# Weight-slice scales from sums of squares on ScalarE, and the last y tiles kept in PSUM, in an attention and two-MoE kernel

## The chip, the cores and the metric

The kernel runs on one core of one Trainium2 chip. The metric is the device time of one execution in microseconds; lower is better. Five engines work side by side, each through its own instructions in a fixed order: PE (matmuls), DVE (vector), ACT (scalar), POOL (general) and SP, which here only starts DMAs. An instruction that waits stops everything behind it on its engine.

## The reference

Attention over 4 batches of 8 heads (576 positions, width 64), then two feed-forward layers on 2304 tokens of width 512:

```python
def _moe_ref(x, w_in, w_out, s, b):            # w_in 512x2048
    r = np.maximum(x @ w_in, 0.0)
    return ((s * (r * r) + b) @ w_out).astype(np.float32)

def _moe2_ref(x, w_a, w_b, w_out):             # w_a, w_b 512x1536
    return (((x @ w_a) * (x @ w_b)) @ w_out).astype(np.float32)

def reference(...):                            # attention -> x [2304, 512]
    x = _moe_ref(x, **moe_kwargs)
    return _moe2_ref(x, **moe2_kwargs)
```

## The kernel before

**Order.** The kernel is not run through loops on the chip. At build time each step is declared with `op(engine, cost, prio, fn, r, w, ...)`: an engine, a planned duration, a due time (smaller is earlier), what it reads and writes. A list scheduler (`Plan`) then fixes the order of each engine from these costs, due times and the number of free buffers. A planned duration that differs from the real one makes no error, only an order that fits less well.

**Stages.** Tokens form 9 chunks of 256. Attention and the first MoE run chunk by chunk up to about 498 us of the span. `last_two` then runs the first MoE for the last two chunks together: 16 slices of hidden units (hh, L987) are folded into four output tiles `yy0` to `yy3` in PSUM (L999), each 128 x 512, where 256 columns belong to chunk 7 and 256 to chunk 8. In the kernel before, a tile is read by DVE for its largest absolute value (L1006), copied to SBUF (L1012, two on ACT and two on DVE), stored to DRAM (L1015) and loaded again where it is used (L1200, L1237).

**The first half of MoE 2** (L1246, from 586 us) computes x @ w_a and x @ w_b in six slices `i` of 256 hidden units. For each slice, each of the two weights `m` and each of two blocks `j` of four chunks, `group` runs seven products, as in Strassen's scheme: 11, d2, d1, 21, d3, d4, 22. A product is `mm6`, six matmuls of 128x512 in fp16. The products share three PSUM banks: b1 takes 11 and then 21 on top, b2 takes d2, d3, d4, and b3 takes d1, 22. Between two products on one bank, a partial result must have been read from it: ACT copies b1 to `su` (L1298), DVE adds b2 to it (L1284, `su`, `u3`, `at_all`), for m = 1 DVE also multiplies (L1291). The product that comes next on the bank waits for that read. The ninth chunk goes without Strassen: `conv` runs two halves of 12 smaller matmuls for each slice and weight (banks `bc`). Of x, the kernel keeps pieces `x011` to `x0d4` (block 0), `x111` to `x1d4` (block 1) and `xc` (ninth chunk), each an fp16 high part (ACT, L1179) and a low part (DVE, L1180) scaled by `xsc`; the differences for block 1 are made on POOL (L1209). `x_scale` gets `xsc` through one small matmul `xbank` (L1101) and five tiny DVE operations (L1105 to L1109).

**Weight slices.** `w2_slice` prepares 18 slices of 1 MB: 12 of w_a and w_b (names like `raw2_03`: weight 0, slice 3) and 6 of w_out (`raw2_o1`). Each is loaded (L459) and decoded in three passes over 128x1024: a Prelu on ACT (L463), a shift, on DVE (L472) for one half of the slices and on ACT (L468) for the other, and a combination on DVE (L474). Then come sums of blocks (L1137), and for the 12 slices the largest absolute value on DVE (L1143), a matmul `wbank` over the partitions in PE's own queue (L1147), two tiny DVE operations (L1151, L1152), and the splits into `wa` and `ws` (ACT L1160, DVE L1166).

**The second half** (`pb`, L1490, from 849 us) multiplies the products a*b, reloaded from DRAM, by w_out.

Of the kernel before, what the change touches and what calls it, by code (L numbers as in the profile page):

```python
# [238 lines left out]
def fused_kernel(  # L239
# [845 lines left out]
    def x_scale(z, t_bank, pos):  # L1085
        i, sc = 10 + z, xsc[:, z]
        both = [(ymax_b, c) for c in ((0, 1, 2, 3) if z == 2 else (4, 5, 6, 7))]

        def tail():
            c0 = 0 if z == 2 else 4  # L1090
            nc.vector.tensor_reduce(out=ymax[:, 9:10], in_=ymax[:, c0 : c0 + 4], axis=AX.X, op=ALU.max)
            if z == 2:
                nc.vector.tensor_tensor(out=ymax[:, i : i + 1], in0=ymax[:, 9:10], in1=ymax[:, 9:10], op=ALU.mult)
            else:
                nc.vector.tensor_tensor(out=ymax[:, 9:10], in0=ymax[:, 9:10], in1=ymax[:, 9:10], op=ALU.mult)
                nc.vector.tensor_tensor(out=ymax[:, i : i + 1], in0=ymax[:, 9:10], in1=ymax[:, 8:9], op=ALU.add)
# [603 lines left out]
```

## Time and profile before

| what | value |
|---|---|
| median of 3 runs | 989.39 us (985.68 to 991.02) |
| the profiled execution's own time | 988.24 us |
| its span | 986.3 us |
| TensorE clock granted over the span, share of full | 0.996 |
| attention and first MoE of chunks 0 to 6 | 0 to about 498.7 us |
| first MoE of the last two chunks | 498.7 to 586.5 us |
| MoE 2, first half (L1246) | 586.5 to 849.0 us |
| MoE 2, second half (L1490, L1550) | 849.0 to 986 us |

The profile is one execution. Times in its rows are microseconds from the start of the span; the device time has 1.9 us around the span. In a row of a timeline, what stands in square brackets is the idle time of the engine just before, and the instruction whose end released it.

### The profile page before, as it was taken

The page shows a single profiled execution, that of the slowest core. Times are in us where ns is not written, and L with a number is a line of the kernel's source. Part 1 is how long each engine was busy: PE and PEld are TensorE (multiplying, and loading weights), DVE is VectorE, ACT ScalarE, POOL GpSimd, SP SyncE. Part 2 cuts the span into 40 slices and gives each one's busy share as a digit, 9 for nine tenths or more (in the row PEclk, how much of TensorE's full clock was granted, in tenths as well). Part 3 has the DMA queues.
Part 4 walks back from the last instruction along what each step waited for, and adds up shares of the span by engine and source line. Part 5 has one row for each costly group of instructions (what it writes and reads, how often), then busy time and mean ns, then how long its engine had stood idle before and what let it go on. Part 6 is the DMA issues. An engine that isn't in the chain of part 4 may idle for free.

```text
span 986.3 us, 16813 instructions
## 1 busy us (share of the span) xinstructions
PE 945.5 (96%) x6361; PEld 765.0 (78%) x6361; DVE 743.6 (75%) x1221; ACT 548.0 (56%) x1009; POOL 159.4 (16%) x228
## 2 busy tenths in 40 slices
PE   5799999999999999999999998998999999999998
PEld 4698998999999999999978873554554544688888
DVE  6878665677978888888487548789687886878852
ACT  4788984567878787877464424343253431334431
POOL 4112003210201102003031004124132411000000
PEclk9999999999999999999999999999999999999999
DMA  8969555447788778776541113547256657976012
GB/s 251 225 162 242 178 205 126 92 133 157 159 175 153 172 150 187 139 166 137 137 160 59 43 49 106 175 156 261 98 197 210 244 203 282 395 291 236 22 67 104
DMA packets 161552, 165.34 MB, mean 168 GB/s; under 512 B 115264, under 2 KB 126272, under 8 KB 155584
## 3 DMA queue, kind: packets, MB, share of 16 engines
q1 hardware_dynamic: 161472, 164.28, 58.4%
q8 instruction: 50, 0.82, 0.3%
q14 instruction: 30, 0.25, 0.1%
HBM read 100.44 MB, written 37.52 MB: 140 GB/s over the span
## 4 chain that ended last, share of the span: by engine, by line
PE 73%; DVE 12%; DMA 8%; issue 3%; ACT 2%; POOL 1%; SPq 1%; DVEq 0%; POOLq 0%; ACTq 0%
PE h L931 14%; PE y L951 13%; PE b L1246 12%; PE pb L1490 11%; PE yy L999 4%; PE av L593 4%; PE hh L987 4%; PE s L643 2%; PE s L829 2%; PE bc L1246 2%; PE pbc L1550 2%; DMA tr<-hl 2%; DVE at_all L1291 1%; DMA raw<-in_w_dram 1%; DMA raw<-in_w2ab_dram 1%
## 5 line engine op out<-in xcount | busy, mean ns | idle before, releaser
L951 PE MATMUL y<-g,w 128*128 128x256 f32 x1344 | 181.3, 286 | 2.0 <-ACT p L659 2.0
L931 PE MATMUL h<-x_all,w 128*128 128x256 f32 x1344 | 179.1, 287 | 1.4 <-ACT x_all L604 0.6
L931 PEld LDWEIGHTS h<-x_all,w 128*128 128x128 f32 x1344 | 168.9, 194 | 2.7 <-ACT x_all L604 0.8
L951 PEld LDWEIGHTS y<-g,w 128*128 128x128 f32 x1344 | 167.7, 192 | 3.9 <-ACT p L659 2.2
L1246 PEld LDWEIGHTS <-wa 128*128 128x128 f16 x720 | 70.2, 99 | 64.1 <-issue 9.4
L1246 PEld LDWEIGHTS <-ws 128*128 128x128 f16 x576 | 56.3, 98 | 69.8 <-issue 4.3
L553 ACT ACTIVATE hl<-p,rc 128x256 f16<-128x256 f32 (+3 forms) x128 | 64.7, 557 | 20.2 <-DVE rc L570 9.7
L1246 PE MATMUL b<-x,wa 128*128 128x512 f16 x288 | 69.8, 379 | 1.2 <-ACT su L1298 0.7
L555 DVE SCALAR_TENSOR_TENSOR hl<-p,rc,hl 128x256 f16<-128x256 f32 (+3 forms) x128 | 66.4, 565 | 3.3 <-ACT hl L553 3.2
L881 ACT ACTIVATE r<-h 128x512 f32<-128x512 f32 x56 | 33.1, 591 | 52.6 <-PE h L931 52.5
L593 PE MATMUL av<-tr,vt 128*64 128x320 f16 (+4 forms) x800 | 48.1, 275 | 10.1 <-DMA tr<-hl 9.5
L593 PEld LDWEIGHTS <-vt 128*64 128x64 f16 (+1 forms) x800 | 40.8, 117 | 18.3 <-issue 7.2
L1246 PE MATMUL b<-x1d,ws 128*128 128x512 f16 x216 | 51.7, 379 | 2.1 <-DVE su L1284 1.5
L1490 PE MATMUL pb<-g,wo 128*128 128x512 f32 x216 | 50.8, 390 | 1.6 <-DVE g L1438 1.6
L643 PE MATMUL s<-kq 66*128 66x256 f32 (+1 forms) x128 | 42.4, 458 | 10.5 <-POOL vt L374 7.7
L1246 PE MATMUL b<-x0d,ws 128*128 128x512 f16 x216 | 51.3, 379 | 0.0
L892 DVE SCALAR_TENSOR_TENSOR r<-r,sb_s 128x512 f32<-128x512 f32 x40 | 30.1, 752 | 27.4 <-ACT r L881 27.0
L1298 ACT COPY su<-b 128x512 f32<-128x512 f32 x24 | 14.0, 583 | 64.7 <-PE b L1246 57.0
L1490 PEld LDWEIGHTS pb<-g,wo 128*128 128x128 f32 x216 | 40.4, 188 | 10.4 <-DVE g L1438 2.1
L987 PE MATMUL hh<-x_all,w 128*128 128x512 f32 x192 | 46.3, 391 | 1.1 <-DMA x_all<-xl_dr 1.1
L999 PE MATMUL yy<-gg,w 128*128 128x512 f32 x192 | 45.8, 389 | 0.0
L1284 DVE TENSOR_TENSOR su<-b,su 128x512 f32<-128x512 f32 x48 | 32.7, 685 | 15.8 <-PE b L1246 15.5
(408 smaller groups left out, 1853.5 us busy)
## 6 DMA issues: line engine op xcount, KB each, us to landing
raw<-in_w_dram SPq DMA_DIRECT2D x16, 1024.0 KB
raw<-in_w2ab_dram SPq DMA_DIRECT2D x12, 1024.0 KB
ab_dr<-at_all SPq DMA_DIRECT2D x24, 512.0 KB
R<-ab_dr SPq DMA_DIRECT2D x24, 512.0 KB
wo<-wo_dr SPq DMA_DIRECT2D x12, 1024.0 KB
rk<-in_k_dram SPq DMA_DIRECT2D x16, 576.0 KB
raw_o<-in_w2o_dram SPq DMA_DIRECT2D x6, 1024.0 KB
wo_dr<-wao SPq DMA_DIRECT2D x24, 256.0 KB
```

What stands on the lines that cost most here:

```text
L553: nc.scalar.activation(o, i_, AF.Copy, scale=r_)
L555: nc.vector.scalar_tensor_tensor(out=o, in0=i_, scalar=r_, in1=place()[:, k0:k1, 0, :cols], op0=ALU.mult, op1=ALU.subtract)
L593: nc.tensor.matmul(ap.t[64 * h : 64 * h + 64, :w], vap(j, h, vi), t[:, j, a, h, :w], start=j == 0 and m == 0, stop=j == nkt - 1 and m == l ...
L643: nc.tensor.matmul(o, qt[:66, x, h, ti * P : (ti + 1) * P], kt[:66, x, h, :w], start=True, stop=False)
L881: op(ACT, 0.49, e, lambda: nc.scalar.activation(r.t.rearrange("p a n -> p (a n)"), hp.t, AF.Relu), r=[hp], w=[r], late=0.1)
L931: nc.tensor.matmul(o, w[:, wi, c, :], x_t[ck, c].t[:, xi], start=m == 0, stop=m == 3 * KC - 1)
L951: nc.tensor.matmul(o, w1_t[2 * fp + j].t[:, 1, wi, e * P : (e + 1) * P], g.t[:, gi, j], start=fp == 0 and e % 2 == 0 and j == wi == gi == ...
L987: nc.tensor.matmul(hp.t, w[:, wi, c, :], x_all[:, :, c, xi, :], start=m == 0, stop=m == 3 * KC - 1)
L999: nc.tensor.matmul(y_ps[e].t, w1_t[f].t[:, 1, wi, e * P : (e + 1) * P], g.t[:, gi].rearrange("p a n -> p (a n)"), start=f == m == 0, stop= ...
L1246: nc.tensor.matmul(o, wt.t[:, q, wi, kt * P : (kt + 1) * P], hl_of(kt, xi), start=first and n == 0, stop=last and n == 5, skip_group_check ...
L1284: op(DVE, 0.64, e, lambda: nc.vector.tensor_tensor(out=dst(), in0=bank.t, in1=a(), op=ALU.add), r=[bank, *reads], w=[key], late=0.08)
L1490: nc.tensor.matmul(banks[bi][dp].t, wv(i2, wi, dp), hl.t[:, i2, xi, :], start=n_ in fresh and ip == i2 == m == 0, stop=ip == NIP - 1 and i ...
```

## The change

- The scale of a weight slice comes from a sum of squares: ACT runs Square over 128x1024 with a sum along the row (L1132 of the changed file) and DVE casts the sum (L1135), in place of DVE's reduction. Behind `wbank`, four tiny DVE operations (L1142 to L1145) stand in place of two.
- The shift runs on ACT (L468) for all 18 slices.
- The tiles `yy0` to `yy3` are neither reduced on DVE nor copied nor stored. ACT runs Square on each in PSUM with a sum (L1007), and one scale serves all of block 1 and the ninth chunk: one `xbank`, one set of five tiny operations (L1094 to L1098). `xc` is split from PSUM in four pieces of 128x256 (L1172, L1173). For block 1, DVE copies the chunk-7 half of each tile (L1202, four of 128x256) beside the rest, which is loaded from DRAM with an earlier due time; two of the four go to a buffer `yw` that takes a weight slot.
- `xc` and the pieces of block 1 have other due times, `back` makes one factor per slice and scale, and ten planned durations differ.

The diff, cut to its core:

```diff
@@ last_two
-                    op(DVE, DVE_PS(512), pr - M, lambda e=e: nc.vector.tensor_reduce(
-                        out=ymax[:, 0:8].rearrange("p (c e) -> p c e", c=2)[:, :, e],
-                        in_=y_ps[e].t.rearrange("p (c n) -> p c n", c=2), axis=AX.X, op=ALU.max, apply_absolute_value=True
-                    ), r=[y_ps[e]], w=[(ymax_b, e), (ymax_b, 4 + e)], late=0.1)
-                    yo = Buf(t_r, f"yyo{e}")
-                    eng, f_ = (DVE, nc.vector.tensor_copy) if e % 2 else (ACT, nc.scalar.copy)
-                    op(eng, 0.6, pr - M, lambda f_=f_, yo=yo, e=e: f_(yo.t.rearrange("p a n -> p (a n)"), y_ps[e].t),
...
-                        op(SP, 0.4, pr - M, lambda i=i, e=e, ck=ck, yo=yo: nc.sync.dma_start(
...
+                    sq = Buf(t_r, f"yyq{e}")
+                    op(ACT, 0.75, pr - M, lambda sq=sq, e=e: nc.scalar.activation(
+                        sq.t.rearrange("p a n -> p (a n)"), y_ps[e].t, AF.Square, accum_out=xsc[:, 6 + e : 7 + e]
+                    ), r=[y_ps[e]], w=[sq, (xsc_b, 6 + e)], late=0.1)
@@ x_scale
-    x_scale(1, t_y, 600.0)
-    x_scale(2, t_y, 601.0)
+    x_scale(1, t_h, 600.0)
@@ w2_slice
-        words = decode(raw, src, n % 2 == 1, pos, pos)
+        words = decode(raw, src, True, pos, pos)
...
-            op(DVE, 1.2, pos, lambda: nc.vector.tensor_reduce(
-                out=sc.t[:, 2:3].bitcast(BF16)[:, 0:1], in_=words(1).bitcast(F32), axis=AX.XY, op=ALU.max, apply_absolute_value=True
-            ), r=[(raw, "hi")], w=[(sc, "m")])
+            op(ACT, 1.3, pos, lambda: nc.scalar.activation(
+                words(0).bitcast(F32), words(1).bitcast(F32), AF.Square, accum_out=sc.t[:, 2:3]
+            ), r=[(raw, "hi")], w=[(sc, "q"), (raw, "lo")])
+            op(DVE, 0.1, pos, lambda: nc.vector.tensor_copy(sc.t[:, 3:4].bitcast(BF16)[:, 0:1], sc.t[:, 2:3]),
+               r=[(sc, "q")], w=[(sc, "m")])
...
-                nc.vector.tensor_scalar(sc.t[:, 1:2], bank.t[:, :1], VSC / XSC, 1e-18, op0=ALU.mult, op1=ALU.max)
-                nc.vector.reciprocal(sc.t[:, 0:1], sc.t[:, 1:2])
+                nc.vector.tensor_scalar(sc.t[:, 2:3], bank.t[:, :1], VSC, 1e-30, op0=ALU.mult, op1=ALU.max)
+                nc.vector.tensor_scalar(sc.t[:, 1:2].bitcast(I32), sc.t[:, 2:3].bitcast(I32), -0.5, 1597463007.0, op0=ALU.mult, op1=ALU.add)
+                nc.vector.tensor_scalar(sc.t[:, 0:1], sc.t[:, 1:2], XSC, None, op0=ALU.mult)
+                nc.vector.reciprocal(sc.t[:, 1:2], sc.t[:, 0:1])
...
-            op(ACT, 1.08, pos + k_, hi, r=[rd, *reads], w=[(t, 0)])
-            op(DVE, 1.12, pos + k_, lo, r=[rd, (t, 0), *reads], w=[(t, 1)])
+            op(ACT, 1.12, at + k_, hi, r=[rd, *reads], w=[(t, 0)])
+            op(DVE, 1.27, at + k_, lo, r=[rd, (t, 0), *reads], w=[(t, 1)])
@@ x_pair
+                    op(SP, 0.35, 530.0 if j else pr, lambda at=at, T=T, e=e, n=n: nc.sync.dma_start(at()[:, :n], y_dr.t[2 * j + T, e, :, :n]),
+                       r=y_rows(2 * j + T, e), w=[(t, k_)], dma=n * 512)
+                    if n == N:
+                        op(DVE, 0.37, 575.0, lambda at=at, e=e: nc.vector.tensor_copy(at()[:, N:], y_last[e].t[:, N:]),
+                           r=[y_last[e]], w=[(t, k_)], late=0.1)
@@ x_conv
-        for e in (0, 2):
-            raw = Buf(t_yraw, f"yrc{e}")
-            src = lambda raw=raw: raw.t[:, :, :N]
-            op(SP, 0.35, pos, lambda src=src, e=e: nc.sync.dma_start(src(), y_dr.t[u, e : e + 2, :, :N].rearrange("e p n -> p e n")),
-               r=[(y_dr, (2 * u, e + z)) for z in range(2)], w=[raw], dma=262144)
-            split2(raw, lambda e=e: half(e, 0), (X["c"], e, lambda e=e: half(e, 1)), src, pos, 2)
+        for e in range(KC):
+            split2(y_last[e], lambda e=e: part(e, 0), (X["c"], e, lambda e=e: part(e, 1)), lambda e=e: y_last[e].t[:, :N], pos, 1, 0.5)
@@ group, times, conv
-            op(PE, 1.37, M + pr + z, lambda: mm6(bank.t, wt, q, x, lambda kt, xi: x.t[:, kt, xi], first, last),
+            op(PE, 1.30, M + pr + z, lambda: mm6(bank.t, wt, q, x, lambda kt, xi: x.t[:, kt, xi], first, last),
...
-            op(DVE, 0.64, e + 0.1, lambda: nc.vector.scalar_tensor_tensor(
+            op(DVE, 0.72 if rd is b1 else 0.82, e + 0.1, lambda: nc.vector.scalar_tensor_tensor(
...
-            op(PE, 1.44, M + pr + fh, go, r=[wa, x], w=[(bank, fh)], late=0.15)
+            op(PE, 1.31, M + pr + fh, go, r=[wa, x], w=[(bank, fh)], late=0.15)
@@ the calls
-    x_pair(1, BASE + 1.0)
-    x_conv(BASE + 2.0)
+    x_conv(590.0)
+    x_pair(1, 590.0)
```

Three places show how the orders differ. The first is DVE where the stage of L1246 has just begun. `su000`, `u3000` and `b2000` belong to slice 0, weight 0, block 0; `xc` and `x111` are pieces of x. Before:

```order
L1284 TENSOR_TENSOR su000_7500<-b2000_7479,su000_7500 128x512
L1105 TENSOR_SCALAR xsc_88<-xbank1_7518 128x1
L1106 TENSOR_SCALAR xsc_88<-xsc_88 128x1
L1107 TENSOR_SCALAR xsc_88<-xsc_88 128x1
L1108 TENSOR_TENSOR xsc_88<-xsc_88 128x1
L1109 RECIPROCAL xsc_88<-xsc_88 128x1
L1105 TENSOR_SCALAR xsc_88<-xbank2_7520 128x1
L1106 TENSOR_SCALAR xsc_88<-xsc_88 128x1
L1107 TENSOR_SCALAR xsc_88<-xsc_88 128x1
L1108 TENSOR_TENSOR xsc_88<-xsc_88 128x1
L1109 RECIPROCAL xsc_88<-xsc_88 128x1
L1180 SCALAR_TENSOR_TENSOR x111_7541<-yr100_7299,xsc_88,x111_7541 128x512
```

and of the changed kernel:

```order
L1283 TENSOR_TENSOR su000_7504<-b2000_7488,su000_7504 128x512
L1094 TENSOR_SCALAR xsc_88<-xbank1_7515 128x1
L1095 TENSOR_SCALAR xsc_88<-xsc_88 128x1
L1096 TENSOR_SCALAR xsc_88<-xsc_88 128x1
L1097 TENSOR_TENSOR xsc_88<-xsc_88 128x1
L1098 RECIPROCAL xsc_88<-xsc_88 128x1
L1173 SCALAR_TENSOR_TENSOR xc_7535<-yy0_6932,xsc_88,xc_7535 128x256
L1173 SCALAR_TENSOR_TENSOR xc_7535<-yy1_6936,xsc_88,xc_7535 128x256
L1283 TENSOR_TENSOR u3000_7551<-b2000_7488,su000_7504 128x512
L1173 SCALAR_TENSOR_TENSOR xc_7535<-yy2_6946,xsc_88,xc_7535 128x256
L1283 TENSOR_TENSOR at_all_7540<-b3000_7489,u3000_7551 128x512
```

The second set of scale operations is gone; the addition `u3000` stands behind two pieces of `xc` where it stood behind one piece of `x111`.

The second place is DVE's queue about slice 2, weight 1, block 0 (`b2200`), where weight slices 12 and 03 are prepared. Before:

```order
L1284 TENSOR_TENSOR su200_8233<-b2200_8213,su200_8233 128x512
L1284 TENSOR_TENSOR su111_8175<-b2111_8156,su111_8175 128x512
L1170 TENSOR_TENSOR wso1_8245<-smo1_8165,wso1_8245 128x4x256
L1284 TENSOR_TENSOR su111_8175<-b3111_8157,su111_8175 128x512
L1291 SCALAR_TENSOR_TENSOR at_all_7549<-su111_8175,wsc01_7080,at_all_7549 128x512 x2
L1166 SCALAR_TENSOR_TENSOR wa12_8256<-raw2_12_8108,wsc12_8208,wa12_8256 128x4x256
L472 TENSOR_SCALAR raw2_03_8210<-raw2_03_8210 128x1024
L474 SCALAR_TENSOR_TENSOR raw2_03_8210<-raw2_03_8210 128x1024
L1284 TENSOR_TENSOR u3200_8320<-b2200_8213,su200_8233 128x512
L1143 TENSOR_REDUCE wsc03_8324<-raw2_03_8210 128x1
```

and of the changed kernel:

```order
L1142 TENSOR_SCALAR wsc12_8222<-wbank12_8257 128x1
L1143 TENSOR_SCALAR wsc12_8222<-wsc12_8222 128x1
L1144 TENSOR_SCALAR wsc12_8222<-wsc12_8222 128x1
L1145 RECIPROCAL wsc12_8222<-wsc12_8222 128x1
L1283 TENSOR_TENSOR u3200_8286<-b2200_8182,su200_8199 128x512
L1283 TENSOR_TENSOR at_all_7540<-b3200_8183,u3200_8286 128x512
L1159 SCALAR_TENSOR_TENSOR wa12_8291<-raw2_12_8135,wsc12_8222,wa12_8291 128x4x256
L1283 TENSOR_TENSOR at_all_7540<-b2200_8182,su200_8199 128x512
L1283 TENSOR_TENSOR at_all_7540<-b3200_8183,su200_8199 128x512
L474 SCALAR_TENSOR_TENSOR raw2_03_8242<-raw2_03_8242 128x1024
```

The addition `u3200` now stands ahead of the split of `wa12` and of slice 03's decoding, and the shift L472 is no longer in the row.

The third place is ACT's queue at the same slice 03. In the changed kernel:

```order
L463 ACTIVATE raw2_03_8242<-raw2_03_8242 128x1024
L1345 COPY ac2_8314<-bc20_8272 128x512
L468 ACTIVATE raw2_03_8242<-raw2_03_8242 128x1024
L1155 CAST wso1_8324<-smo1_8202 128x4x256
L1297 COPY su210_8350<-b1210_8326 128x512
L1132 ACTIVATE raw2_03_8242,wsc03_8365<-raw2_03_8242 128x1024
L1297 COPY su201_8402<-b1201_8382 128x512
```

and before:

```order
L1160 ACTIVATE wa12_8256<-raw2_12_8108,wsc12_8208 128x4x256
L463 ACTIVATE raw2_03_8210<-raw2_03_8210 128x1024
L1305 COPY at_all_7549<-b1200_8212 128x512
L1160 ACTIVATE ws12_8326<-sm12_8267,wsc12_8208 128x4x256
L1298 COPY su210_8335<-b1210_8311 128x512
```

Two passes of slice 03, L468 and L1132, now stand on ACT between its Prelu and the copies `su210` and `su201`, which free the b1 banks.

## Rows read from the trace of the kernel before

**Rows 1.** the page's first part: busy time (share of the span) and instructions

```profile
PE 945.5 (96%) x6361; PEld 765.0 (78%) x6361; DVE 743.6 (75%) x1221; ACT 548.0 (56%) x1009; POOL 159.4 (16%) x228
```

**Rows 2.** stretches A:B: length, busy us of each engine, PEclk, DMA share, GB/s

```profile
586.40:633.00 46.60, 42.67 (x221) 21.21 (x221) 38.99 (x66) 18.94 (x27) 12.40 (x10) 1.00 0.35 119
...
633.00:849.00 216.00, 210.60 (x1091) 106.42 (x1089) 171.34 (x225) 79.88 (x90) 58.40 (x80) 0.99 0.62 220
```

**Rows 3.** timeline of PE: start, us, work, [idle before <- releaser]

```profile
604.10 1.24 PE L1246 MATMUL b<-x0d,wa 128*128 128x512 f16 x5 [1.87 <-DVE u L1284]
...
631.67 1.46 PE L1246 MATMUL b<-x,ws 128*128 128x512 f16 x6
...
632.96 0.81 PE L1246 MATMUL b<-x,wa 128*128 128x512 f16 x3
...
652.09 1.24 PE L1246 MATMUL b<-x1d,wa 128*128 128x512 f16 x5 [0.78 <-DVE u L1284]
...
672.60 1.24 PE L1246 MATMUL b<-x1d,ws 128*128 128x512 f16 x5 [0.87 <-DVE su L1284]
...
688.02 0.81 PE L1246 MATMUL b<-x0d,wa 128*128 128x512 f16 x3 [2.04 <-DVE u L1284]
...
764.36 0.81 PE L1246 MATMUL b<-x1d,wa 128*128 128x512 f16 x3 [1.07 <-DVE u L1284]
...
848.98 1.40 PE L1490 MATMUL pb<-g,wo 128*128 128x512 f32 x5
...
856.57 0.73 PE L1490 MATMUL pb<-g,wo 128*128 128x512 f32 x2 [1.64 <-DVE g L1438]
```

**Rows 4.** a stretch, same columns, about the wait at 688.02

```profile
688.00:694.00 6.00, 5.98 (x26) 3.30 (x26) 3.69 (x5) 1.64 (x2) 2.96 (x4) 0.72 0.31 122
```

**Rows 5.** timeline of DVE ahead of 688.02

```profile
683.03 1.86 DVE L1166 SCALAR_TENSOR_TENSOR wa<-raw,wsc,wa 128x1024 f16<-128x1024 f32 x1
684.81 1.23 DVE L472 TENSOR_SCALAR raw<-raw 128x1024 uint32<-128x1024 uint32 x1
686.14 1.23 DVE L474 SCALAR_TENSOR_TENSOR raw<-raw 128x1024 uint32<-128x1024 uint32 x1
687.28 0.68 DVE L1284 TENSOR_TENSOR u<-b,su 128x512 f32<-128x512 f32 x1
```

**Rows 6.** groups, 480 to 860: xcount | busy us, mean ns | idle before

```profile
L1143 DVE TENSOR_REDUCE wsc<-raw 128x1 bf16<-128x1024 f32 x12 | 14.6, 1216 | 0.2
...
L468 ACT ACTIVATE raw<-raw 128x1024 uint32<-128x1024 uint32 x6 | 6.9, 1144 | 0.0
...
L472 DVE TENSOR_SCALAR raw<-raw 128x1024 uint32<-128x1024 uint32 x6 | 5.0, 828 | 7.1 <-DMA raw<-in_w2ab_dram 7.1
...
L472 DVE TENSOR_SCALAR raw_o<-raw_o 128x1024 uint32<-128x1024 uint32 x3 | 2.1, 684 | 0.0
...
L1152 DVE RECIPROCAL wsc<-wsc 128x1 f32<-128x1 f32 x12 | 2.0, 165 | 0.4
...
L1147 PE MATMUL wbank<-wsc,total 128*128 128x1 bf16 x12 | 2.0, 168 | 0.1
...
L1246 PE MATMUL b<-x,wa 128*128 128x512 f16 x288 | 69.8, 379 | 1.2 <-ACT su L1298 0.7 <-DVE x L1180 0.5
```

**Rows 7.** groups as before, whole span: sums along a row, and Square

```profile
L849 ACT ACTIVATION_READ_ACCUMULATOR p<-s,nm 128x1 f32 x64 | 12.4, 194 | 0.0
...
L884 ACT ACTIVATE r<-r 128x512 f32<-128x512 f32 x16 | 10.1, 629 | 0.2
```

**Rows 8.** timeline of ACT at the scale of block 1

```profile
591.16 0.72 ACT L1179 ACTIVATE x<-yr,xsc 128x512 f16<-128x512 f32 x1 [1.35 <-DVE xsc L1107]
591.90 0.58 ACT L1305 COPY at_all<-b 128x512 f32<-128x512 f32 x1
```

**Rows 9.** groups, 200 to 600: a split of 128x256 out of PSUM

```profile
L604 ACT ACTIVATE x_all<-av,vsc 128x256 fp32r<-128x256 f32 x16 | 7.5, 468 | 2.0 <-PE av L593 1.6
```

**Rows 10.** waits, 586 to 860: us in total, times, longest us

```profile
ACT raw L463 <- DMA raw<-in_w2ab_dram: 10.9, 6, 3.0
```

More of the change, by code (lines that the diff above doesn't have):

```diff
@@ L1023, in last_two @@
                 y_slice(f - Y_LAG, pos(f) + 0.1)
+        return y_ps
     def chunk_units(cks, pos):
@@ L1058, in fused_kernel @@
     t_wv.queue = t_w.queue
+    t_yw = Tag(lambda n: t_w.make(n).rearrange("p a b n -> p (a b n)").bitcast(F32).rearrange("p (a b n) -> p a b n", a=2, b=2), NF1, True, t_w)
+    t_yw.queue = t_w.queue
     t_sum = tag("ph2", [P, 4, 2 * P], F32, 1, "wsum")
@@ L1085, in x_scale @@
     def x_scale(z, t_bank, pos):
-        i, sc = 10 + z, xsc[:, z]
-        both = [(ymax_b, c) for c in ((0, 1, 2, 3) if z == 2 else (4, 5, 6, 7))]
+        i, sc = 10 + z, xsc[:, 3 * z : 3 * z + 3]
         def tail():
[L1090 to L1096, printed above, removed]
+            nc.vector.tensor_reduce(out=xsc[:, 10:11], in_=xsc[:, 6:10], axis=AX.X, op=ALU.add)
+            nc.vector.tensor_tensor(out=ymax[:, i : i + 1], in0=xsc[:, 10:11], in1=ymax[:, 8:9], op=ALU.add)
         if z:
-            op(DVE, 0.3, pos, tail, r=[*both, *([(ymax_b, 8)] if z == 1 else [])], w=[(ymax_b, i)])
+            op(DVE, 0.3, pos, tail, r=[(ymax_b, 8), *((xsc_b, 6 + e) for e in range(KC))], w=[(ymax_b, i)])
         bank = Buf(t_bank, f"xbank{z}")
@@ L1186, in y_rows @@
     def y_rows(u, e):
-        return [(y_dr, (ck, e // 2 if ck < NCK - 2 else e)) for ck in (2 * u, 2 * u + 1) if ck < NCK]
+        return [(y_dr, (ck, e // 2)) for ck in (2 * u, 2 * u + 1) if ck < NCK - 2]
     def x_pair(j, pos):
+        yw = Buf(t_yw, f"yw{j}") if j else None
         for n_ in NAMES:
@@ L1195, in x_pair @@
             r = {}
+            both = yw if kt else None
             for kh in range(2):
-                t = Buf(t_yraw, f"yr{j}{kt}{kh}")
+                t = both or Buf(t_yraw, f"yr{j}{kt}{kh}")
                 for T in range(2):
-                    r[kh, T] = (t, T), lambda t=t, T=T: t.t[:, T]
-                    op(SP, 0.35, pr, lambda t=t, T=T, e=2 * kh + kt: nc.sync.dma_start(t.t[:, T], y_dr.t[2 * j + T, e]),
-                       r=y_rows(2 * j + T, 2 * kh + kt), w=[(t, T)], dma=262144)
+                    k_ = (kh, T) if both else T
+                    at = lambda t=t, kh=kh, T=T, both=both: t.t[:, kh, T] if both else t.t[:, T]
+                    r[kh, T] = (t, k_), at
+                    e = 2 * kh + kt
+                    n = N if j and T else 2 * N
+                    op(SP, 0.35, 530.0 if j else pr, lambda at=at, T=T, e=e, n=n: nc.sync.dma_start(at()[:, :n], y_dr.t[2 * j + T, e, :, :n]),
[3 more added lines that the diff above has]
+                           r=[y_last[e]], w=[(t, k_)], late=0.1)
             def split(n_, k_, kt=kt, r=r, pr=pr):
@@ L1207, in sub @@
             def sub(o, a, b, r=r, pr=pr):
-                eng, f_, cost = (POOL, nc.gpsimd, 1.2) if j else (DVE, nc.vector, 0.65)
+                eng, f_, cost = (POOL, nc.gpsimd, 1.45) if j else (DVE, nc.vector, 0.75)
                 op(eng, cost, pr, lambda: f_.tensor_tensor(out=r[o][1](), in0=r[a][1](), in1=r[b][1](), op=ALU.subtract),
@@ L1348, in conv @@
             ac = ac_t[i]
-            un = back(i, 2, e)
+            un = back(i, 1, e)
             op(DVE, 0.64, e, lambda: nc.vector.scalar_tensor_tensor(
-                out=ac.t, in0=bank.t, scalar=un.t[:, 6:7], in1=ac.t, op0=ALU.mult, op1=ALU.mult
+                out=ac.t, in0=bank.t, scalar=un.t[:, 5:6], in1=ac.t, op0=ALU.mult, op1=ALU.mult
             ), r=[bank, (un, 2)], w=[ac], late=0.08)
```

38 lines of the change are left out of this document (18 added, 20 removed).

## The prediction

> **What bounds the kernel now.** The page's busy line comes first [rows 1]: PE is busy for 945.5 of 986.3 us, so time can only be won from PE's remaining 41 us, or lost by adding waits. Next come the stretches, since the edits touch only those after 586 us (and, in their preparation, the 90 us before, where the first slices are made). In 586.4 to 633.0 PE is busy for 42.67 of 46.60 us, in 633 to 849 for 210.60 of 216 [rows 2]. DVE is busy for 171.34 of those 216 us and ACT for only 79.88; DVE is the engine that is close to full beside PE, and ACT has room.
>
> What a piece of work costs on PE shows in its timeline: two products follow each other at 631.67 and 632.96 [rows 3], 1.29 us from start to start, and conv halves take as long. The first stretch holds 28 products and 4 halves (four groups of seven; slice 0 of the ninth chunk twice), 32 x 1.295 = 41.4, with small matmuls 41.6; its length is 46.5, so **4.9 us** are lost. The second holds 140 products and 20 halves, 160 x 1.295 = 207.2, with ten small matmuls 207.7, of 216.0: **8.3 us** lost. More than 13.2 us plus the 1.64 us at 856.57 [rows 3] can't be won by edits here.
>
> Then, wait by wait, who is late [rows 3]: DVE's partial additions L1284, with 1.87 us at 604.10, 0.78 at 652.09, 0.87 at 672.60, 2.04 at 688.02 and 1.07 at 764.36 (smaller ones stand between them). At 604 and at 652, d3 and d4 stand directly one after the other on bank b2 in PE's order, so the addition between them is PE's wait whenever DVE is late at all. The row ahead of 688.02 shows the mechanism [rows 5]: L1166 at 683.03, L472 at 684.81, L474 at 686.14, each 1.2 to 1.9 us, all for weight slices that are needed later; the addition that PE waits for starts at 687.28 behind them. There is a second price: in 688 to 694 the granted clock averages 0.72 [rows 4], and the engine had just been idle for 2 us, its longest wait in this stage. Part of the stretch ran at the lower level, 1.2 GHz. It costs 6.0 x 0.28 = **1.7 us**.
>
> **The change part by part.**
>
> *DVE loses work.* Twelve reductions L1143 at 1.216, 14.6 us; nine shifts L472, 5.0 + 2.1 us [rows 6]; at the tiles of the last two chunks four reductions and two copies of 128x512 out of PSUM, by an addition of that shape (0.68 [rows 5]) about 4 us more. It gains, per slice, a cast and two tiny operations at about 0.16 each (as L1152 [rows 6]), 12 x 0.48 = 5.8, and four copies of 128x256, at most the 0.468 of a split of that shape [rows 9], 1.9 us. Net about -18 us between 498 and 849.
>
> *ACT gains work.* A Square over 128x1024 doesn't exist in the trace. Its nearest rows are the ACT pass over the same shape, 1.144 [rows 6], plus reading out a sum, 0.194 [rows 7]: 1.34; twelve are 16.1. Nine shifts at 1.144 make 10.3. Four Squares of y tiles at 0.629 + 0.194 = 0.82 [rows 7] stand for two copies. In all some 28 us onto an engine that is busy for 99 of the 262 us from 586 to 849: it goes to about 48%. Work on DVE or ACT is off the path unless a partial read that PE waits for stands behind it; so these sums price nothing by themselves, and I follow the waits.
>
> *Transition, 586 to 633.* Before, the scales take two sets of tiny operations; ACT's first split that needs the scale starts at 591.16, behind 1.35 us of idle time [rows 8]. After, one xbank in the same place of PE's queue gives the scale at the same time. ACT then splits xc piece 0 (0.468 [rows 9], to 591.65), copies at_all (0.58 [rows 8], its bank is ready; to 592.5 with the hand-overs) and splits xc piece 1 (to 592.95). DVE makes its low half (0.5, to 593.5) and only then u3000 (0.69, to 594.2), since the order puts u3000 behind two xc pieces. d4 of the group, third product after xbank (at 590.4, 591.7, due at 593.0), so waits until 594.25: **a new wait of 1.25**. Beyond that place, conv's 24 small matmuls now stand between d3 and d4 of b2010, where the 1.87 arose, and block 1's pieces no longer need a store and a load through DRAM. I keep that wait and nothing else: 4.9 - 1.25 = about -3.7. Bounds: -4.1 if u3000 is late by only 0.8 (ACT's hand-overs at their shortest), -2.6 if by 2.3 (the 1.87 of 604.10 with a split of 0.468 more).
>
> *Steady part, 633 to 849.* The order shows that u3200 now stands ahead of the split of wa12 and of slice 03's decoding: the 2.04 goes, and with it the 1.7 of the clock. For 652, 672 and 764 DVE's queue in the changed order has 0.55 us or more of spare time ahead of each addition, when I lay the durations of the rows one after the other. Named waits are 0.78 + 0.87 + 2.04 + 1.07 = 4.8, with the clock 6.5, of the 8.3; the other 1.8 are small pieces that I leave standing. A new order brings small waits of its own; I take 1.0 for these, about half of what stands now. **-5.5.** Bounds: -8.3 (all) and about 0 (the copies on ACT become late instead; below).
>
> *The end.* The 1.64 at 856.57 waits for DVE's split L1438, which the edits don't touch: 0. Bounds: -1.64, and +1 for a shifted load. Before 586, one ACT pass and one Square more for each of two slices lie beside 90 us of matmuls; hidden.
>
> **Sum:** -3.7 - 5.5 = -9.2 against the profiled execution's 988.24, that is 979.0. That execution lies 1.15 under the median, so on the median's scale 989.39 - 9.2 = **980.2**.
>
> **The rivals.**
>
> *All of the loss goes:* 989.39 - 13.2 - 1.64 = 974.5. For it speaks that planned durations are closer to the rows (a product 1.30 against 1.29 measured); against it the order's own 1.25.
>
> *A: ACT takes DVE's place as the late engine.* ACT waits six times for the landing of a slice, 10.9 us together, 3.0 at most [rows 10]. Whatever stands behind such a Prelu on ACT, copies `su` included, is late with it; and now two passes of 1.14 and 1.34 stand between them and the copies. If each of the six late landings costs PE one more pass, 6 x 1.144 = 6.9, then 980.2 + 6.9 = 987.1: no change. Against it: before, with the same six waits ahead of them, the copies `su` cost PE 0.7 in all [rows 6]. The Trainium skill, page "ScalarE: Activation LUTs", section "Rules for kernel authors", says to put relu, max, min, add and mul on VectorE rather than ScalarE; the shift, 0.684 to 0.828 on DVE against 1.144 on ACT [rows 6], agrees, and by that rule this change makes work dearer (9 x 0.36, some 3 us) and ends like A. It counts work and not who is waited for, so I leave it a rival.
>
> *B: wbank becomes a wait, slower.* PE executes wbank in its queue; before, the twelve never waited (idle before: 0.1 us in all [rows 6]). The chain to it was one reduction of 1.216; now it is a Square of 1.34 behind ACT's other work, a cast of 0.16 and another hand-over of 0.2, and the shift, 0.3 to 0.46 dearer. If the ten wbanks in the steady part stand where nothing is spare, each stalls PE by the ACT pass 1.14 and these additions, up to 1.6: +16, 989.39 - 9.2 + 16 = 996. It cancels the gain from 0.92 each, and is slower by 0.5% from 1.4 each. Against it: the order places wbank by the planner's durations, which now have the Square at 1.3, and I find 1.7 us to spare at the two tightest.
>
> *The change doesn't do what it says* (the order as before) is excluded by the order: reductions, shifts and stores are gone from it.
>
> **How the numbers follow.** A measurement of this kernel can tell about 0.5% from no change: 984.4 and 994.3 are the bounds. The forecast, with both bounds of each term from 976 to 984.4: 0.60. All gone: 0.10. A, with milder forms from 984.5 to 989: 0.22. B: 0.08. Faster 0.70, same 0.22, slower 0.08. The range 974.5 to 988 leaves out B, half of the all-gone case and a little of A: about 0.16.
>
> **What would show it right or wrong.** In PE's timeline: a wait of about 1.2 us near 594, none over 0.6 at the places of 604, 652, 672 and 688, no stretch at half clock near 688, and the first `pb` at 840 instead of 848.98 [rows 3]. In the stretches: ACT near 48% busy, DVE down by some 18 us, PE idle about 1.3 before 633 and 3 after. Wrong by A would be waits of PE for ACT's L1297 behind L468 or L1132; by B, waits of `wbank` for DVE's cast L1135. If DVE is down by 18 us and PE's waits for it remain, then they were waits by order and not by load, and the sum fails at its second term.

## The result

The changed kernel takes 978.41 us (median of 6 runs, 974.54 to 981.65) against 989.40 us (6 runs, 985.68 to 991.02): a ratio of 0.9889 with a 95% interval of 0.9858 to 0.9919, about 11 us faster. The forecast was 980.2 us. The profiled execution took 980.05 us, with a span of 978.0.

First the page's busy line of the changed kernel, which answers to [rows 1]:

```profile
PE 943.5 (96%) x6360; PEld 766.1 (78%) x6360; DVE 725.0 (74%) x1228; ACT 573.0 (59%) x1050; POOL 159.8 (16%) x222
```

DVE lost 18.6 us and ACT gained 25.0, near what was worked out ahead (18 and 28). Next the stretches of the changed kernel, with the columns of [rows 2]; the first half of MoE 2 now ends at 841:

```profile
500.00:502.00 2.00, 1.91 (x6) 1.62 (x7) 2.00 (x4) 2.00 (x3) 1.69 (x5) 0.72 0.47 167
502.00:504.00 2.00, 2.00 (x6) 1.52 (x6) 1.01 (x2) 0.63 (x2) 1.92 (x2) 0.50 0.03 10
...
633.00:841.00 208.00, 208.00 (x1091) 105.89 (x1090) 159.54 (x237) 95.90 (x113) 58.38 (x75) 1.00 0.64 224
```

From 633 on PE is busy for 208.00 of 208 us, where it was 210.60 of 216. And PE's timeline of the changed kernel, which answers to [rows 3]:

```profile
500.09 7.32 PE L987 MATMUL hh<-x_all,w 128*128 128x512 f32 x24 [2.56 <-DMA x_all<-xl_dr]
...
589.11 1.47 PE L1242 MATMUL b<-x,wa 128*128 128x512 f16 x6
...
596.66 1.46 PE L1242 MATMUL b<-x0d,wa 128*128 128x512 f16 x6 [0.87 <-DVE u L1283]
...
610.10 1.46 PE L1242 MATMUL b<-x0d,wa 128*128 128x512 f16 x6 [1.60 <-DVE u L1283]
...
841.11 5.94 PE L1489 MATMUL pb<-g,wo 128*128 128x512 f32 x25
...
848.38 1.88 PE L1489 MATMUL pb<-g,wo 128*128 128x512 f32 x7 [1.33 <-DVE g L1437]
```

The stage begins at 589.11 and ends at 841.11: **252.00 us**, where it was 848.98 - 586.46 = 262.52. It won 10.5 us. The part after it won 0.4. The part ahead of it lost 2.65 in this pair of profiles: PE waited 2.56 us for x at 500.09, where it had waited 1.08, and a stretch at the lower clock followed, 0.72 and then 0.50 in the rows above, which is 1.2 GHz. So 10.5 + 0.4 - 2.65 = 8.3 us between the two spans. The length of that wait differs from execution to execution: three kernels below keep the changed kernel's order on PE from end to end, and they wait 0.88, 0.97 and 1.13 us there. It comes again in the last experiment. The length of the stage is a sharper measure than the total: four kernels below have PE's order of the changed one in this stage, and two of them take 252.00 as well, the others 252.19 and 252.59, while single totals of one kernel differ by 7 to 10 us. But each length is that of one execution, and a stretch at the lower clock within the stage makes it 1.7 us longer (in the kernel before, behind 688; below, in old_dur and dur_only). Both measures are given.

### The profile page after: what moved, and what is told of

The parts are those of the page before. It is cut to its first block, busy times and chain, and to the rows that moved or that the text cites. A ratio compares the mean times of both kernels' runs of the same rounds, so it can differ in the third digit from the quotient of the medians.

```text
span 978.0 us, 16832 instructions
## 1 busy us (share of the span) xinstructions
PE 943.5 (96%) x6360; PEld 766.1 (78%) x6360; DVE 725.0 (74%) x1228; ACT 573.0 (59%) x1050; POOL 159.8 (16%) x222
## 4 chain that ended last, share of the span: by engine, by line
PE 88%; DMA 6%; DVE 3%; ACT 1%; issue 1%; POOL 1%; SPq 0%; POOLq 0%; DVEq 0%
PE b L1242 21%; PE h L931 16%; PE y L951 14%; PE pb L1489 11%; PE hh L987 5%; PE yy L999 4%; PE av L593 4%; PE s L643 3%; PE bc L1242 3%; PE s L829 3%; DMA tr<-hl 2%; PE pbc L1549 2%; DMA x_all<-xl_dr 1%; DMA raw<-in_w_dram 1%; DMA R<-ab_dr 1%
```

## Which part carries the gain

The theory with which the experiments began was that DVE had been relieved: 18 us less for it to do, so the additions that PE waits for are on time. The rival was that the planned durations, closer to the real ones, gave a better order, whatever DVE has to do.

Four runs each undo one part of the change and let the planner order anew.

**undo_square** (the reduction on DVE again):

```diff
-            op(ACT, 1.3, pos, lambda: nc.scalar.activation(
-                words(0).bitcast(F32), words(1).bitcast(F32), AF.Square, accum_out=sc.t[:, 2:3]
+            op(DVE, 1.2, pos, lambda: nc.vector.tensor_reduce(
+                out=sc.t[:, 2:3].bitcast(BF16)[:, 0:1], in_=words(1).bitcast(F32), axis=AX.XY, op=ALU.max, apply_absolute_value=True
```

> The changed kernel with one part undone: the twelve scales of weight slices come from DVE's reduction again, with two tiny operations behind wbank; everything else as changed, and the order planned anew. Theory (DVE relieved at a few places): DVE gets about 9 us back between 498 and 841, and some of the partial additions stand behind a reduction of 1.22 again; 2 to 4 us of the 10.5 won in the first half of MoE 2 are lost, 980 to 982. Rival (the corrected planned durations alone make the order fit): within 1 us of the changed kernel, 978 to 979.

**undo_shift**:

```diff
-        words = decode(raw, src, True, pos, pos)
+        words = decode(raw, src, n % 2 == 1, pos, pos)
```

> The changed kernel with one part undone: nine of the eighteen shifts run on DVE again (0.68 to 0.83 us each, 7 us together), the order planned anew. Theory (DVE relieved): 1 to 3 us lost, 979.5 to 981.5, with one or two waits of PE for L1283 after 640. Rival (planned durations alone): within 1 us of the changed kernel. Rival (ScalarE is the dearer engine for this pass): faster than the changed kernel by 1 to 3 us, since ACT loses 10 us.

**undo_y** (the kernel before, with the Squares, the shifts on ACT and the new durations; its `last_two`, `x_pair` and `x_conv` are those of before):

```diff
-            op(DVE, 1.2, pos, lambda: nc.vector.tensor_reduce(
+            op(ACT, 1.3, pos, lambda: nc.scalar.activation(
...
-        words = decode(raw, src, n % 2 == 1, pos, pos)
+        words = decode(raw, src, True, pos, pos)
...
-            op(PE, 1.37, M + pr + z, lambda: mm6(
+            op(PE, 1.30, M + pr + z, lambda: mm6(
```

> The changed kernel with one part undone: the last y tiles are reduced on DVE, copied, stored and loaded through DRAM again, with two scales; Squares of weight slices, shifts and planned durations stay. Theory: this part is worth only what the transition shows, where the changed kernel loses 2.8 us and the kernel before 4.9: about 2 us slower than changed, 980 to 981, and the stretch after 640 stays free of waits. Rival (the tiles' path carries the gain): 4 us or more slower.

**old_dur**:

```diff
-            op(PE, 1.30, M + pr + z, lambda: mm6(
+            op(PE, 1.37, M + pr + z, lambda: mm6(
...
-            op(PE, 1.31, M + pr + fh, go,
+            op(PE, 1.44, M + pr + fh, go,
```

> The changed kernel with the old planned durations (a product 1.37, a conv half 1.44, the splits, sums and multiplications as before); the work is the changed kernel's. Theory (DVE relieved): the planner orders a little worse, 1 to 3 us lost, 979.5 to 981.5. Rival (the durations are what made the order fit): most of the gain goes, 984 to 988, with waits of PE for L1283 of 1 to 2 us after 640.

Then **dur_only** puts the new durations alone into the kernel before (the same lines the other way round):

> The kernel before with the new planned durations alone; its work is unchanged. Theory (DVE relieved at a few places): the order is a little better, but DVE has as much to do: 1 to 4 us faster than before, 985 to 988. Rival (the durations are what made the order fit): 7 us or more faster, 979 to 982, and the wait of 2.04 with the half clock behind it is gone.

Each ratio is to runs of the kernel before that were taken on the same chip beside it.

| kernel | median, us | ratio to before (95%) | first half of MoE 2 |
|---|---|---|---|
| before | 989.40 | 1 | 262.52 |
| changed | 978.41 | 0.9889 (0.9858 to 0.9919) | 252.00 |
| undo_square | 979.17 | 0.9918 (0.9886 to 0.9950) | 253.50 |
| undo_shift | 983.77 | 0.9940 (0.9911 to 0.9968) | 257.23 |
| undo_y | 982.85 | 0.9938 (0.9911 to 0.9965) | 255.71 |
| old_dur | 983.25 | 0.9943 (0.9918 to 0.9967) | 258.51 |
| dur_only | 984.64 | 0.9967 (0.9953 to 0.9982) | 254.50 |

In the stage, the undone parts cost 1.5, 5.2, 3.7 and 6.5 us, together 16.9, more than the 10.5 that there were to lose. The parts don't add up: each run is a new order. The total of undo_square can't be told from the changed kernel's; the medians of the other three lie 4.4 to 5.4 us above it.

Held against the expectations: undo_square lost 0.8 us in all, as the rival had it, and 1.5 in the stage, between the two. undo_shift lost 5.4, more than any of its three theories allowed. undo_y lost 4.4, which is its rival's 4 or more, and the stretch after 640 didn't stay free of waits. old_dur came out at 983.25, beyond the theory's 981.5 and a little under the rival's 984; its profile shows the slowest of its ten runs (987.42), with a stretch at the lower clock at 607 (0.72 in 606 to 612), so its 258.51 is more than its median speaks for.

What each lost shows in PE's timeline. Of undo_square:

```profile
754.68 1.46 PE L1238 MATMUL b<-x1d,wa 128*128 128x512 f16 x6 [1.28 <-DVE u L1279]
```

This is the theory's wait, but one. Of undo_shift:

```profile
757.16 1.46 PE L1242 MATMUL b<-x1d,wa 128*128 128x512 f16 x6 [0.78 <-DVE u L1283]
...
763.40 1.04 PE L1242 MATMUL b<-x,wa 128*128 128x512 f16 x4 [3.06 <-DVE wa L1159]
```

and DVE ahead of it:

```profile
756.42 0.69 DVE L1283 TENSOR_TENSOR u<-b,su 128x512 f32<-128x512 f32 x1 [0.54 <-PE b L1242]
...
760.74 1.40 DVE L1290 SCALAR_TENSOR_TENSOR at_all<-su,wsc,at_all 128x512 f32<-128x512 f32 x2
762.06 1.28 DVE L1159 SCALAR_TENSOR_TENSOR wa<-raw,wsc,wa 128x1024 f16<-128x1024 f32 x1
```

The largest wait is not for an addition behind a long pass but for the low half of a weight slice that stands behind additions and multiplications. DVE had nothing to do for 0.54 us ahead of 756.42, and no shift stands between there and 762.06: that is a bad place, and not the load of 7 us of shifts. Of old_dur:

```profile
607.70 2.72 PE L1242 MATMUL b<-x0d,ws 128*128 128x512 f16 x6 [2.45 <-DVE su L1283]
...
624.12 1.46 PE L1242 MATMUL b<-x,wa 128*128 128x512 f16 x6 [1.66 <-ACT su L1297]
...
749.52 1.46 PE L1242 MATMUL b<-x,ws 128*128 128x512 f16 x6 [1.44 <-DVE u L1283]
```

With DVE relieved as in the changed kernel, additions and a copy are late all the same. In undo_y the steady part keeps two waits of 0.78, and the transition has waits of 0.81, 1.39 and 1.08 for DVE, where the kernel before has 1.87, 0.48 and 0.60.

In dur_only the planned durations alone bring 8.0 of the 10.5 us in the stage, though every reduction and shift is still on DVE:

```profile
640.00:740.00 100.00, 100.00 (x529) 51.17 (x528) 82.45 (x109) 42.01 (x47) 31.14 (x44) 1.00 0.57 198
740.00:835.00 95.00, 94.86 (x485) 47.03 (x484) 78.43 (x104) 31.36 (x35) 25.14 (x32) 1.00 0.65 235
```

The waits at 652, 672, 688 and 764 of [rows 3] are gone while DVE is busy for 82 of 100 us. Of the 2.5 us that are missing, 1.7 are a stretch at the lower clock in the transition, behind a wait of 1.27 for a piece of x at 609.50:

```profile
608.00:614.00 6.00, 4.73 (x15) 1.71 (x14) 4.79 (x6) 3.45 (x6) 3.69 (x3) 0.72 0.59 228
```

The total won only 3.4 us of its own `before` (988.04), so it lies in the theory's range, while the stage speaks for the rival; the gain is given back where the second half begins. PE's timeline of dur_only there:

```profile
841.67 3.23 PE L1490 MATMUL pb<-g,wo 128*128 128x512 f32 x13
...
851.55 4.37 PE L1490 MATMUL pb<-g,wo 128*128 128x512 f32 x11 [2.46 <-DVE g L1438]
```

and its stretch:

```profile
846.00:860.00 14.00, 11.40 (x41) 8.65 (x42) 13.22 (x13) 6.73 (x8) 0.00 (x0) 0.88 1.04 407
```

PE arrives 7.3 us sooner and finds DVE's split L1438 behind three sums L1452, with waits of 1.18 and 2.46 and a clock of 0.88 (14 x 0.12 = 1.7 us). From the first `pb` to the end it takes 983.4 - 841.7 = 141.7 us, the kernel before 137.3. The changed kernel, whose order there differs, has one wait of 1.33 and takes 136.9.

## DVE's load with the order kept

The next three runs keep PE's order of the changed kernel instruction by instruction and change only what the engines have to do.

**reduce_load**:

```diff
+                nc.vector.tensor_copy(sc.t[:, 3:4].bitcast(BF16)[:, 0:1], sc.t[:, 2:3])
+                nc.vector.tensor_reduce(
+                    out=sc.t[:, 7:8].bitcast(BF16)[:, 0:1], in_=words(1).bitcast(F32), axis=AX.XY, op=ALU.max, apply_absolute_value=True)
```

> The changed kernel, its order kept, with DVE's old reduction over 128x1024 added behind each of the twelve casts (1.22 us each, 14.6 together; its result is not used, and the planner doesn't know of it). Load theory (DVE's time is what counts): the waits for additions come back, 4 to 8 us slower than the changed kernel, 982 to 986. Order theory (the additions now stand ahead of the long passes): 2 us or less, since only additions with under 1.2 us to spare behind a cast become late.

**old_work** issues the reductions and nine shifts on DVE, in ops that the planner still counts for ACT:

```diff
-            op(ACT, 1.3, pos, lambda: nc.scalar.activation(
+            op(ACT, 1.3, pos, lambda: nc.vector.tensor_reduce(
...
+            op(ACT, 1.07, pr, (lambda: nc.vector.tensor_scalar(lo(), lo(), 29, None, op0=ALU.logical_shift_right)) if on_dve else (
```

> The changed kernel with its order on PE kept instruction by instruction, but with DVE's work of before: the reductions in place of the Squares and nine shifts are issued on DVE at the places where the planner, which doesn't know of it, had put them for ACT (+22 us for DVE, -26 us for ACT, less the small operations). The y tiles stay in PSUM. Order theory (the places of the passes decide, DVE's hours don't): the first half of MoE 2 takes 252 to 255 us as in the changed kernel, 978 to 981 in all. Load theory (DVE relieved): 4 to 8 us of waits for L1283 come back, 982 to 987.

**square_twice**:

```diff
+                for c in (6, 2):
+                    nc.scalar.activation(words(0).bitcast(F32), words(1).bitcast(F32), AF.Square, accum_out=sc.t[:, c : c + 1])
```

> The changed kernel, its order kept, with each of the twelve Squares of a weight slice executed twice (1.15 + 0.19 us more on ACT each, 16 together, and every cast and wbank later by as much). If ACT and the chain to wbank have room (1.7 us to spare at the tightest wbank by the rows, as the prediction had it): 0 to 2 us slower. Rivals A and B of the prediction (ACT late for the copies, or wbank a wait in PE's queue): 8 to 16 us slower, with waits of PE for L1297 or for L1135.

| kernel | median, us | ratio to before (95%) | first half of MoE 2 |
|---|---|---|---|
| reduce_load | 978.93 | 0.9898 (0.9861 to 0.9935) | 252.59 |
| old_work | 977.66 | 0.9887 (0.9857 to 0.9917) | 252.19 |
| square_twice | 975.16 | 0.9880 (0.9851 to 0.9908) | 252.00 |

None can be told from the changed kernel. The stretch 633 to 835 of old_work

```profile
633.00:835.00 202.00, 202.00 (x1057) 102.59 (x1056) 162.80 (x218) 78.31 (x88) 58.11 (x75) 1.00 0.63 221
```

and the same stretch of the kernel before

```profile
633.00:835.00 202.00, 196.60 (x1008) 98.35 (x1007) 162.59 (x214) 74.92 (x84) 58.40 (x80) 0.99 0.59 209
```

settle it: DVE is busy for 162.8 and 162.6 us, the same, and PE waits for nothing in the one and 5.4 us in the other. reduce_load has one wait there:

```profile
745.34 1.46 PE L1247 MATMUL b<-x1d,wa 128*128 128x512 f16 x6 [0.42 <-DVE u L1288]
```

With this order the load theory falls: 14.6 us more on DVE cost 0.6 us in the stage, the reductions and nine shifts put back on DVE 0.2, and 16 us more on ACT nothing. What is left as the cause is the order, that is, which passes stand ahead of which additions. That it comes down to the passes ahead of the additions that PE needs next is read from the rows at 688 [rows 5]; no run moved one such pass by itself.

Two runs fill the table of work against durations. **work_only** is the kernel before with the Squares and all shifts on ACT and nothing else:

```diff
-            op(DVE, 1.2, pos, lambda: nc.vector.tensor_reduce(
+            op(ACT, 1.3, pos, lambda: nc.scalar.activation(
...
-        words = decode(raw, src, n % 2 == 1, pos, pos)
+        words = decode(raw, src, True, pos, pos)
```

> The kernel before with the Squares and the shifts on ACT, but with the old planned durations and the y tiles through DRAM. Load theory (DVE relieved): most of the gain, the first half of MoE 2 at 253 to 256 us, 980 to 984. Order theory (the planned durations decide): the first half keeps waits of 1 us and more after 640 and takes 258 to 263 us, 985 to 990.

**dur_y** is the changed kernel with both moves to ACT undone (the diffs of undo_square and undo_shift together):

> The changed kernel with both moves to ACT undone (reductions and nine shifts on DVE, planned as such); the y tiles stay in PSUM and the planned durations are new. Order theory: the planner finds an order about as good, the first half of MoE 2 at 252 to 256 us, and the whole is 978 to 982. Load theory: the first half at 257 us or more, 983 to 987. The run with the shifts alone undone took 257.2 in that half, through one late split of a weight slice; if this one is free of such a wait, that was an accident of one order.

work_only: 983.02 us, ratio 0.9926 (0.9899 to 0.9954), stage 255.50. dur_y: 978.78 us, ratio 0.9894 (0.9866 to 0.9921), stage 254.00. So the new durations and the y tiles do without the two moves of work to ACT: dur_y's total can't be told from the changed kernel's, and the 3.06 us of undo_shift were an accident of one order. work_only came out as the load theory had it, in the stage and in all: with the old durations, the moved passes by themselves give an order without the late waits too, save one of 0.62; the transition keeps 4.3 us of waits, 1.87 the longest:

```profile
606.44 1.46 PE L1250 MATMUL b<-x0d,wa 128*128 128x512 f16 x6 [1.87 <-DVE u L1288]
...
752.25 1.46 PE L1250 MATMUL b<-x1d,wa 128*128 128x512 f16 x6 [0.62 <-DVE u L1288]
```

Its order is a new one on PE and DVE alike, so it doesn't tell load from order, as old_work does. Both the shorter queue and the better durations can lead the planner to a good order, and for the steady part one of them is enough. Whether in the order of before, kept, the moved passes would have been enough wasn't tried; an estimate from [rows 5] for its longest wait is that without L472, 1.23 us of the work ahead of the addition, 0.8 of the 2.04 would be left.

## Two waits that are left

**subs_dve** tries the 1.60 us at 610.10:

```diff
-                eng, f_, cost = (POOL, nc.gpsimd, 1.45) if j else (DVE, nc.vector, 0.75)
+                eng, f_, cost = DVE, nc.vector, 0.75
```

> The changed kernel with the eight differences of x for block 1 on DVE in place of POOL (L1211). In the changed kernel the splits L1173 of block 1 take 1.4 to 1.8 us while POOL is busy with these, against 0.74 at other times, and PE waits 1.60 us at 610.10 behind three of them. Theory (DVE and POOL slow each other): the splits take 0.75, DVE has 5.5 us more of its own but about 4 us less of slowed work, and the wait at 610 shrinks to under 0.6: 1 us faster than the changed kernel. Rival (the long splits are slow by themselves, or wait for their operands): they stay at 1.4 and PE waits longer, 2 to 4 us slower.

It takes 977.22 us, ratio 0.9889 (0.9867 to 0.9911), stage 252.56: no gain. In the changed kernel DVE runs ahead of 610 like this:

```profile
603.99 1.44 DVE L1173 SCALAR_TENSOR_TENSOR x<-yw,xsc,x 128x512 f16<-128x512 f32 x1
605.36 1.76 DVE L1173 SCALAR_TENSOR_TENSOR x1d<-yr,xsc,x1d 128x512 f16<-128x512 f32 x1
607.03 1.75 DVE L1173 SCALAR_TENSOR_TENSOR x<-yw,xsc,x 128x512 f16<-128x512 f32 x1
...
609.37 0.68 DVE L1283 TENSOR_TENSOR u<-b,su 128x512 f32<-128x512 f32 x1
```

beside POOL, which is busy without a pause:

```profile
604.96 1.60 POOL L1211 TENSOR_TENSOR yr<-yr 128x512 f32<-128x512 f32 x1
606.53 3.39 POOL L1211 TENSOR_TENSOR yw<-yw 128x512 f32<-128x512 f32 x2
```

With POOL's subtractions moved to DVE, the groups of subs_dve read

```profile
L1173 DVE SCALAR_TENSOR_TENSOR x<-yr,xsc,x 128x512 f16<-128x512 f32 x9 | 6.6, 745 | 0.0
...
L1173 DVE SCALAR_TENSOR_TENSOR x1d<-yr,xsc,x1d 128x512 f16<-128x512 f32 x4 | 3.0, 742 | 0.0
```

So POOL's work does slow the splits, from 0.745 to as much as 1.76; that half of the theory holds. The Trainium skill, page "SBUF — State Buffer", section "Who interferes with whom", says that a DVE instruction with two inputs in SBUF and a GpSimd instruction that reads SBUF get in each other's way; these rows agree. The wait at 610 went, but a piece of x for block 1 is now late by 1.40 and a copy by 0.60. PE's order differs by six matmuls, and the late piece stands on DVE behind a multiplication (L1349) that itself waited 0.73 us for `conv`; how much of the 1.40 is the subtractions' time on DVE isn't shown:

```profile
612.95 1.89 PE L1242 MATMUL b<-x,wa 128*128 128x512 f16 x8 [1.40 <-DVE x L1173]
615.44 2.75 PE L1242 MATMUL b<-x,wa 128*128 128x512 f16 x12 [0.60 <-ACT su L1297]
```

**x_first** is about the wait for x ahead of the stage:

```diff
-        words = decode(raw, src, True, pos, pos)
+        words = decode(raw, src, True, pos, pos, xl_loads if i == 0 and scaled else ())
```

> The changed kernel with one thing more: the loads of weight slices 00 and 10 (2 MB, needed at 586) are issued behind the four loads of x for the last two chunks (L875), where they stood ahead of them. In the traces so far PE waits for these loads at about 498, from 0.65 to 2.56 us, and the longer of these waits have a stretch at half clock behind them. Theory (the 2 MB ahead of them make them late): the wait goes and with it the half clock, 1 to 4 us faster than the changed kernel, 974 to 977, and a smaller spread of the runs. Rival (the round trip through DRAM sets the wait, not the traffic): no change, 978.

It takes 976.77 us (975.87 to 980.18), ratio 0.9873 (0.9847 to 0.9899), and PE's timeline has no wait at that place:

```profile
490.04 5.92 PE L952 MATMUL y<-g,w 128*128 128x256 f32 x48
495.80 5.63 PE L988 MATMUL hh<-x_all,w 128*128 128x512 f32 x24
501.27 3.04 PE L952 MATMUL y<-g,w 128*128 128x256 f32 x24
```

The planner has also moved these 24 matmuls of hh ahead of the last 24 of the chunk before (y), so x was needed some 3 us earlier and was there. The DMA issues, first of the changed kernel, then of x_first:

```profile
485.09 0.51 SPq L610 DMA_DIRECT2D xl_dr<-xl  x1
...
487.72 0.90 SPq L459 DMA_DIRECT2D raw<-in_w2ab_dram  x2
488.72 3.07 SPq L875 DMA_DIRECT2D x_all<-xl_dr  x4
```

```profile
486.40 0.51 SPq L610 DMA_DIRECT2D xl_dr<-xl  x1
...
489.16 1.74 SPq L876 DMA_DIRECT2D x_all<-xl_dr  x4
490.95 1.11 SPq L459 DMA_DIRECT2D raw<-in_w2ab_dram  x2
```

From the issue of the last store of x to the first matmul on it are 15.0 us in the changed kernel (500.09) and 9.4 in x_first (495.80). All thirteen other kernels waited there, for 0.65 to 2.56 us, and this one doesn't; so the 2 MB ahead made x late, and the rival, the round trip, falls. That the total is faster than the changed kernel's is not shown: 1.6 us between the medians lie inside the intervals, and the stage of the profiled execution begins at 586.55, no earlier than old_work's with its wait of 0.88 (586.42). A smaller spread, 4.3 us against 7.1 in six runs each, isn't shown by so few. A wait of 0.32 for a copy on DVE came at 509.44. It is faster than the kernel before beyond doubt, and of the version to keep one can say that it has one wait less.

## Why the prediction was right, point by point

- **What bounds the kernel**: right. PE's waits for L1284 and the clock behind the 2.04 made up the steady loss, and all of it went.
- **What was to be seen**: the first `pb` at 840 came at 841.11, no wait of 0.6 or more is left where 652, 672 and 688 had theirs, and no stretch at the lower clock stands in the stage. ACT is busy for 46% of it (48 forecast). Not seen as forecast: the place of 604, where none over 0.6 was to be left, still has 1.60 (now at 610.10), and PE is idle for 2.5 us before 633 and none after, where 1.3 and 3 were forecast.
- **Steady part, forecast -5.5**: the term was mis-sized; it measured -8.3, the bound. The step that failed is the allowance of 1.0 for small waits of a new order and the 1.8 of small pieces left standing: there are none, 208.00 of 208. Of the 1.8 only 0.6 could be small waits at all, since PE was idle for 5.4 us in that stretch (210.60 of 216) and 4.8 of these are the named ones; the rest went with them. The reading of the order (u3200 ahead of the long passes, 0.55 us to spare at each addition) was what held.
- **Transition, forecast -3.7**: mis-sized the other way, -2.2 (192 pieces take 249.3 us by the sum of the prediction, the stage 252.0, so 2.7 are lost where 4.9 had been). The foreseen wait behind xbank came, with 0.87 instead of 1.25, at 596.66. The step that failed is "I keep that wait and nothing else": the addition u3010, which cost 1.87 at 604.10, was taken to be covered by conv's 24 matmuls, and costs 1.60 behind them at 610.10. On DVE it stands behind splits of block 1, which the sum gave no price at all. Three of them take 1.44, 1.76 and 1.75 beside POOL's subtractions; at the 0.745 of subs_dve they would take 2.7 us less, which is more than the wait, and in subs_dve it is gone. The passes that stand ahead of the addition were left out, and with them what runs beside them.
- **The end, 0**: 1.33 instead of 1.64. But dur_only shows that nothing guards this place: with another order 4.4 us are given back there.
- **Before 586, hidden**: no wait of PE there can be put down to the change. The wait for x (2.56 instead of 1.08), with its stretch at half clock, is one that the same order also made with 0.88 to 1.13.
- **The total**: 978.41 against 980.2. The steady part won 2.8 us more than forecast and the transition 1.5 less; the two errors offset each other in part, so some of the closeness is luck.
- **All of the loss goes (974.5)**: it came true for the steady part and not for the transition and the end.
- **Rival A and B**: both fall with square_twice. ACT with 16 us more, and twelve chains to `wbank` longer by 1.35 each, cost nothing in the stage; B's price of 0.92 each wasn't reached. (What B adds up, 1.14 with 0.12, 0.16, 0.2 and 0.3 to 0.46, is about 2.0 and not 1.6; nothing hangs on it.) A's six late landings are still there, 11.1 us together and 4.2 at most, and PE waits for no copy on ACT. In the changed kernel the group of `wbank` has 0.0 us of idle time ahead of it, and the Square costs what was worked out, 1.153 + 0.194:

```profile
L1132 ACT ACTIVATE raw<-raw 128x1024 f32<-128x1024 f32 x12 | 13.8, 1153 | 1.8 <-DVE raw L474 1.8
L1132 ACT ACTIVATION_READ_ACCUMULATOR raw<-raw 128x1 f32 x12 | 2.3, 194 | 0.0
L1138 PE MATMUL wbank<-wsc,total 128*128 128x1 bf16 x12 | 2.0, 169 | 0.0
```

- **The rule on ScalarE** (the Trainium skill, page "ScalarE: Activation LUTs", section "Rules for kernel authors"): by it, as the prediction read it, the change would have ended like A. The shift is dearer on ACT, as the rule would have it (1.157 against 0.68 to 0.83), and it cost nothing, since nobody waited for it.
- **The cause**: the prediction counted 18 us less for DVE beside the places in its queue, and rightly priced only the places. The theory formed after it, that the relief was the cause, was wrong for this order (old_work).

## What to carry to other kernels

When a change moves work in a kernel that a planner orders, test the work with the order kept before believing that the engine's load was the matter; here the twelve reductions and nine shifts put back on DVE cost 0.2 us in the stage. Price each planned duration by what a trace shows beside its neighbours, since the planner's result hangs on small differences of these, and undoing parts one by one then gives numbers that don't add up. Measure a stage by its own start and end where totals scatter more than the effect, and look whether the clock fell within it.

## What had not been expected of the hardware

A split of 128x512 on DVE took 0.745 us with POOL idle and up to 1.76 beside POOL's subtractions of 128x512. And the clock fell behind some waits and not behind others: after 2.04 us at 688 in the kernel before, 2.56 at 500 in the changed kernel and 1.27 at 609.50 in dur_only it did, after the 3.06 us at 763.40 of undo_shift it didn't, as its stretch shows:

```profile
763.00:769.00 6.00, 5.60 (x26) 2.56 (x27) 2.23 (x3) 1.17 (x2) 3.06 (x4) 1.00 1.06 359
```

The length of a wait alone doesn't tell whether the lower level follows; what does, these runs leave open.
